# The same 722 operations of a two-head kernel, issued in another fixed order

## The chip, the cores and the metric

The kernel runs on one core of one Trainium2 chip. The metric is device time in microseconds (us) for one launch; the figure for a kernel is the median of several runs. A profile is one execution of its own, with its own time.

The engines are named as the profile names them: PE is TensorE's matmul row and PEld its weight loads, DVE is VectorE, ACT is ScalarE, POOL is GpSimd, SP is SyncE. [...] SP issues most of the DMAs here; POOL issues some.

## What is computed

The inputs have sequence length 2048 and width 640 in each of two halves; the output is 2048 x 1280.

```python
# half A: a diagonal complex recurrence between two projections
Bu = einsum("bld,pd->blp", x, B_bar)
h_t = Lam_bar * h_(t-1) + Bu_t
yA = 2 * einsum("blp,dp->bld", h, C).real + x * Dskip
# half B: a short convolution (4 taps), a gate, a long convolution (2048 taps, by FFT), a gate
kv = shift_conv(k) * v
yB = q * (irfft(rfft(kv) * rfft(ssm_k))[:2048] + kv * ssm_D)
```

## The kernel before

**The work is 722 named operations.** `Graph.op` records each with the engines that may run it, the values that it reads and writes, and the buffers that it uses. The string `ORDER` then lists all 722 names in one fixed sequence; `/A`, `/D`, `/G` and `/S` behind a name choose ACT, DVE, POOL or SP where there is a choice. `Graph.place` walks that string, gives each new buffer a slot, and `emit` issues the operations in that sequence. Each engine's program is therefore the sub-sequence of `ORDER` that falls to it.

**Half A.** `B00` to `B11` load B transposed; `xn0`, `xn1` load half of x, `px..` transpose it on PE and `ex..` copy it out; `x1..` load the other half with transposing DMAs. `dn0_j_h`, `dn1_j_h` (line 768, 10 matmuls each) project unit j; `e1_` copies the result out, `m1_` (line 776, 3 matmuls with the tables `set_n_h`) combines four time steps, `e3_` copies that out. `S0`, `S5` with `jw`, `jc`, `js`, `ja`, `scan`, `jv` run the coarse recurrence; `d1_j`/`a1_j` and `d0r_j`/`a0r_j` push it back down to single steps (one or three matmuls, then an addition on DVE). `ct..`/`ect..` build the output weights from C (loaded by `cn..`). `py0_ri` and `py1_ri` (lines 916 and 920, 13 matmuls each) project to the output, `ey_` copies out, `st_` stores.

**Half B** runs for five groups G of 128 channels, as a two-stage DFT written as matmuls. `kG`, `vG` are transposing loads issued by SP; `cv3`, `cs2`, `ca2` to `ca0`, `cm` are the four taps and the gate on ACT and DVE; `kvsG` stores the result to DRAM and `kvlG` loads it back in another layout. `hstG` loads the long filter, `dtapG` adds the skip term, for which `Dm0` clears and `Dm1` loads a small table. `s1h`, `s1k` (line 1019, 32 matmuls each) and `s2h`, `s2k` (line 1055, 16 each) are the forward transforms of filter and signal, each followed by a copy of 128x1024 out of PSUM (`e1h`, `e1k`, `e2h`, `e2k`). `pP`, `pQ`, `pY` multiply on DVE. `i2` (line 1111, 16 matmuls) and its copy `e3G.` begin the inverse, `ztG` is a transposing DMA (line 1118), `i1` (line 1147, 64 matmuls) ends it, `obGh` multiplies with q on DVE, and `obG` stores. `wm`, `ws`, `V` make the DFT tables.

**Buffers.** PSUM has four slots of two banks (tag `P`), and every product above takes one until the copy or addition behind it has read it. SBUF has six large slots (tag `8`) and seven smaller ones (tag `4`). The kernel before picks the slot whose last user ends first by the planner's own clock in `place`.

All copies out of PSUM carry line 350 when ACT does them and line 352 when DVE does; they are told apart by shape.

## Time and profile before

| what | value |
|---|---|
| median of 4 runs | 218.82 us |
| lowest and highest run | 218.65 and 220.35 us |
| the profiled execution: its own time | 220.35 us |
| the profiled execution: span from first to last instruction | 218.2 us |
| PE busy in the span | 194.4 us, 89% |
| DVE, ACT, POOL busy in the span | 175.5, 149.2, 29.0 us |
| 128x1024 copy out of PSUM on ACT, on DVE | 1025 and 1221 ns (83 and 17 of them) |
| SBUF-to-SBUF transpose (line 1118), issue to landing | 7.1 to 9.7 us |

The profiled execution took 2.15 us more than its span, and it is the slowest of the four runs, 1.53 us above their median. "Busy" of PE counts matmuls in flight, not the rate at which they stream. The chain of waits walks back from the last instruction to whatever released each step; "issue" in it is time in which an engine waited for nothing that the profile shows.

### The profile page before, as it was taken

To read this page: it belongs to the slowest core of one execution; us is meant where nothing else is said; L and a number is where in the kernel's file an instruction comes from. 1 tells how busy PE (TensorE), PEld (TensorE's weight loads), DVE (VectorE), ACT (ScalarE), POOL (GpSimd) and SP (SyncE) were. 2 spreads that over 40 slices of the span, in tenths; PEclk is the share of its full clock that TensorE was granted. 3 is DMA by queue.
4 is the path that set the end of the run, shared out by engine and by line. 5 is a ranking of instruction groups with operands and counts; after the bars stand their busy time and mean duration, and the time that the engine had idled before them with its cause. 6 is when DMAs were issued, how large, how long until landed. Compare 5 with 4: busy or idle time off the path is not lost.

```text
span 218.2 us, 8702 instructions
## 1 busy us (share of the span) xinstructions
PE 194.4 (89%) x3947; PEld 138.0 (63%) x3947; DVE 175.5 (80%) x264; ACT 149.2 (68%) x173; POOL 29.0 (13%) x41
## 2 busy tenths in 40 slices
PE   0839999997999799999698999996999989999992
PEld 0737554565765665655564777775777778778871
DVE  7578999889877999899788979955888878988240
ACT  2798689884797999699675675485484788560211
POOL 6116902381100000000000000210000000002020
PEclk9979999999999999999999999997999999999999
DMA  6999957999998443096907956799559980669934
GB/s 191 271 150 182 165 122 112 211 231 154 153 213 181 71 92 62 12 275 130 169 3 147 165 111 157 223 212 220 124 126 187 256 199 10 131 154 142 252 96 125
DMA packets 98751, 33.74 MB, mean 155 GB/s; under 512 B 94842, under 2 KB 96762, under 8 KB 98714
## 3 DMA queue, kind: packets, MB, share of 16 engines
q1 hardware_dynamic: 97580, 29.35, 69.0%
q0 software_dynamic: 1104, 3.84, 7.2%
q8 instruction: 31, 0.51, 1.0%
q14 instruction: 6, 0.05, 0.1%
q10 hardware_dynamic: 30, 0.00, 0.0%
HBM read 9.19 MB, written 7.86 MB: 78 GB/s over the span
## 4 chain that ended last, share of the span: by engine, by line
PE 67%; DVE 11%; ACT 11%; issue 5%; DMA 4%; DVEq 0%; ACTq 0%
PE ps L916 21%; PE ps L768 13%; PE ps L1055 8%; PE ps L1019 7%; PE ps L1147 5%; PE ps L1111 4%; PE ps L869 3%; ACT s L350 3%; DVE s L352 2%; DMA s<-in_A_x_dram 2%; PE ps L920 2%; DMA s<-kvd 2%; ACT xT L350 2%; ACT BC L350 2%; DVE M L535 2%
## 5 line engine op out<-in xcount | busy, mean ns | idle before, releaser
L350 ACT CAST s<-ps 128x1024 bf16<-128x1024 f32 x83 | 79.8, 1025 | 19.9 <-PE ps L1019 9.3
L768 PE MATMUL ps<-xT,BC 128*64 128x512 bf16 x400 | 46.4, 381 | 0.6 <-ACT s L350 0.3
L916 PE MATMUL ps<-BC,hb 128*128 128x320 bf16 x240 | 36.4, 299 | 0.0
L768 PEld LDWEIGHTS <-BC 128*64 128x64 bf16 x400 | 23.1, 110 | 18.7 <-issue 2.2
L1019 PE MATMUL ps<-R,s 64*64 64x128 bf16 x1280 | 24.0, 229 | 10.0 <-issue 4.3
L350 ACT CAST yo<-ps 128x640 bf16<-128x640 f32 x14 | 9.7, 693 | 32.4 <-PE ps L920 21.7
L1019 PEld LDWEIGHTS <-s 64*64 64x64 bf16 x1280 | 21.1, 115 | 13.9 <-issue 7.1
L916 PEld LDWEIGHTS <-hb 128*128 128x128 bf16 x240 | 22.0, 98 | 8.4
L352 DVE CAST s<-ps 128x1024 bf16<-128x1024 f32 x17 | 20.5, 1221 | 6.5 <-PE ps L1019 3.4
L1078 DVE TENSOR_TENSOR s<-s,s 128x2048 bf16<-128x2048 bf16 x20 | 24.4, 1222 | 0.9 <-ACT s L350 0.3
L873 DVE TENSOR_TENSOR hb<-ps,hb 128x512 bf16<-128x512 f32 x30 | 19.8, 686 | 4.7 <-PE ps L869 4.6
L1055 PE MATMUL ps<-s,Wre 128*64 128x128 bf16 x320 | 20.9, 221 | 2.8 <-DVE s L951 1.5
L1055 PEld LDWEIGHTS <-Wre 128*64 128x64 bf16 x320 | 18.0, 109 | 6.5 <-issue 5.3
L994 DVE TENSOR_TENSOR s<-s,s 128x2048 bf16<-128x2048 bf16 x15 | 20.3, 1354 | 0.4
L1055 PE MATMUL ps<-s,Wim 128*64 128x128 bf16 x320 | 20.6, 219 | 0.0
L986 ACT ACTIVATE s<-s,sk 128x2048 bf16<-128x2048 bf16 x9 | 18.1, 2014 | 3.3 <-DVE sk L660 2.5
L1055 PEld LDWEIGHTS <-Wim 128*64 128x64 bf16 x320 | 18.0, 110 | 0.3
L1154 DVE TENSOR_TENSOR s<-ps,s 128x1024 bf16<-128x1024 f32 x10 | 11.9, 1220 | 7.7 <-PE ps L1147 7.7
L350 ACT CAST hb<-ps 128x768 bf16<-128x768 f32 x16 | 12.6, 807 | 3.4 <-PE ps L768 3.4
L1078 DVE TENSOR_TENSOR s<-s 128x1024 bf16<-128x1024 bf16 x20 | 13.8, 689 | 0.3
L916 PE MATMUL ps<-BC,Qb 128*128 128x320 bf16 x80 | 13.0, 313 | 0.0
L988 DVE TENSOR_SCALAR s<-s,sk 128x2048 bf16<-128x2048 bf16 x11 | 12.2, 1117 | 0.1
(160 smaller groups left out, 269.5 us busy)
## 6 DMA issues: line engine op xcount, KB each, us to landing
s<-in_B_q_dram SPq DMA_DIRECT2D x5, 512.0 KB, 4.2
out_dram<-yo SPq DMA_DIRECT2D x15, 160.0 KB, 2.9
kvd<-s SPq DMA_DIRECT2D x4, 512.0 KB, 5.1
s<-kvd SPq DMA_DIRECT2D x4, 512.0 KB, 4.4
s<-in_B_ssm_k_dram POOLq DMA_DIRECT2D x3, 512.0 KB, 8.6
out_dram<-s SPq DMA_DIRECT2D x3, 512.0 KB, 5.5
s<-in_A_x_dram SPq DMA_DIRECT2D x2, 640.0 KB, 5.4
s<-in_B_ssm_k_dram SPq DMA_DIRECT2D x2, 512.0 KB, 4.3
```

Source lines behind the costliest of these rows:

```text
L350: self.nc.scalar.copy(out=out, in_=in_)
L352: self.eng[e].tensor_copy(out=out, in_=in_)
L768: nc.tensor.matmul(P[64 * ri:64 * ri + 64, b, :], lhsT=self.BT[:, k, ri, 64 * j:64 * j + 64], rhs=self.xT[:, k, hf, 2 * b:2 * b + 2, :].re ...
L873: v.tensor_tensor(out=hv(r), in0=self.P(p2)[:, 0, :].rearrange("p (h m) -> p h m", h=2), in1=hv(r), op=ALU.add)
L916: nc.tensor.matmul(P[:, part, 0:320], lhsT=hap(j), rhs=self.CT[:, j, c0:c0 + 320], start=(j == 0), stop=False)
L986: nc.scalar.activation(out=out, in_=k(j), func=ACT.Copy, scale=self.sk[:, G, j:j + 1])
L988: v.tensor_scalar_mul(out=out, in0=k(j), scalar1=self.sk[:, G, j:j + 1])
L994: op(f"ca{j}{G}{h}", {"DVE": dve_tt(W_)}, lambda e, c=c, tt=tt: v.tensor_tensor(out=c(), in0=c(), in1=tt(), op=ALU.add), r=[f"tm{G}{h}"], ...
L1019: nc.tensor.matmul(P[64 * ri:64 * ri + 64, r, 128 * b4:128 * b4 + 128], lhsT=d[64 * r:64 * r + 64, 4 * qd + b4, a0, :], rhs=self.R[64 * r: ...
L1055: nc.tensor.matmul(P[64 * pi:64 * pi + 64, ri, 128 * k4:128 * k4 + 128], lhsT=W[:, kp, pi, :], rhs=A[:, kp + 16 * pi, :], start=True, stop ...
L1078: v.tensor_tensor(out=o, in0=a, in1=b, op=op_)
L1154: v.tensor_tensor(out=o, in0=self.P(pt)[:].rearrange("p s (b a c) -> p a (s b) c", b=8, a=16), in1=o, op=ALU.mult)
```

## The change

The string `ORDER` is another sequence of the same 722 names. No name is added or removed, and no operation's body changes. 36 operations that had a choice move from ACT to DVE and 29 from DVE to ACT; seven table products `set_` change between DVE and POOL (four to POOL, three to DVE), as do three small steps (`kz0` and `dtap4` to POOL, `kz4` to DVE); and the issue of some DMAs moves between SP and POOL (to POOL: `q2`, `q4`, `kvs3`, `kvl4`, `st_01`; to SP: `hst0`, `kvl0`, `kvs1`, `ob3`, `ob4`, `st_32`).

`place` no longer keeps a clock of its own: a new buffer takes a slot never used before, or else the one whose last user stands earliest in the sequence. So the slots differ as well. `schedule` and `better`, which nothing called, are gone, and the constant 0.93 of `i1`, which `place` no longer reads, is 0.98.

The diff, cut to `place` and to the stretches of `ORDER` that are spoken of below:

```diff
         for word in text.split():
             name, _, e = word.partition("/")
             o = ops[name]
             o.eng = letter[e] if e else next(iter(o.alts))
-            assert o.deps <= done, name
-            s = free[o.eng]
-            for d in o.deps:
-                s = max(s, d.end + (0.0 if d.eng == o.eng and not d.dma else (0.3 if d.eng == "PE" else self.SEM)))
+            assert all(d in place for d in o.deps), name
             for b in o.bufs:
                 if b.slot is None:
-                    best = None
+                    ends = []
                     for i, own in enumerate(held[b.tag]):
-                        if own is not None and any(u not in done for u in own.users):
-                            continue
-                        t = 0.0 if own is None else max(u.end for u in own.users) + self.SEM
-                        if best is None or t < best[0]:
-                            best = (t, i)
-                    s = max(s, best[0])
-                    b.slot = best[1]
+                        if own is None:
+                            ends.append((-1, i))
+                        elif all(u in place for u in own.users):
+                            ends.append((max(place[u] for u in own.users), i))
+                    b.slot = min(ends)[1]
                     held[b.tag][b.slot] = b
...
-xn0 ld_lre J0 consts nrow xn1 J1 zero ld_ldt E0 pidx w0 ld_lim c4 nrowf hst1/G B00 E1 wi0 kz0/D bc kz1/G px00 wm0 px02 ex00/A
-px04 Dm0 w1 ex02/A Dm1/G px10 ex04/A par px12 ex10/A px14 p0 ex14/D B01 dtb ex12/A p1 fi w2 nrho ph mk rn k0 R dtap1/G Ct
-s1h10 trig scol s1h11 den s1h12 ld_sk/S e1h10/A rc B10 s1h13 ss e1h11/A dn0_4_0 set_1_0/D set_12_0/G e1h12/A dn1_4_0 B11
-set_1_1/G set_2_0/D e1h13/A dn0_0_0 e1_4_0/A set_2_1/G x100 dn0_1_0 set_3_0/D set_3_1/G dn0_2_0 x101 m1_4_0 sk set_8_1/G
+xn1 ld_lre J0 consts nrow xn0 J1 zero ld_ldt E0 pidx w0 ld_lim c4 nrowf hst1/G B00 E1 kz0/G wi0 bc Dm0 px12 Dm1/G w1 px10
+ex12/A px14 ex10/A wm0 px00 w2 par px02 p0 ex00/D B01 px04 ex14/D dtb mk k0 R ex02/A p1 fi dtap1/G ex04/A s1h13 nrho ph rn Ct
+s1h10 ld_sk/S scol B10 e1h13/D s1h11 trig den dn1_4_0 e1h11/A rc B11 ss e1h10/A dn0_4_0 set_3_0/D set_1_0/G x100 dn0_1_0
+set_2_0/G e1_4_0/D x101 dn0_2_0 sk cs200/D set_8_0/G m1_4_0 v0 cv300/A dn1_2_0 kz1/G set_12_0/D set_3_1/G e3_4_0/A dn0_7_0
...
+e3_7_0/D set_G_1/D dn1_0_1 set_G_0/D diagD dn0_1_1 dn1_1_1 e1_0_1/D kvl0/S hst0/S ws0 cs210/A wi1 m1_0_1 e1_1_1/D dn0_6_0 wm1
+m1_1_1 m1_9_0 e3_9_0/A ws1 v1 dn1_4_1 e3_1_1/D e3_0_1/D e1_6_0/D s1k03 s1k00 e1k03/D dn0_4_1 e1k00/D s1k01 dtap0/G V e1_4_1/A
...
-s1h20 ect40/A s1h21 jcv5 e1h20/A jv5 ect21/D jsv5 s1h22 e1h21/A s1h23 jav50 s1k20 e1h22/A jav51 s1k21 e1h23/D e1k20/A d1_7
-a1_7 d1_8 e1k21/A s1k22 a1_8 d00_7 s1k23 e1k22/A a00_7 d00_8 d1_0 e1k23/A a00_8 d1_1 a1_0 d01_8 s2k20 kz3/G k3 a1_1 s2k21
...
+a1_5 a1_6 ct40 ect31/A a1_7 s2k21 q0/S ect40/A s2k20 e2k21/A ct41 zt0 s2h21 s2h20 ect41/A e2h21/D d00_4 e2k20/A d00_1 a00_4
+d00_2 e2h20/A d00_7 a00_1 d00_0 a00_7 cs230/A d00_6 d00_9 a00_0 d00_5 a00_9 a00_5 s2h22 a00_2 s2h23 e2h22/A a00_6 py0_32
+e2h23/A pP20 i101 zt1 pQ20 py0_03 ob01 py1_03 pY20 i100 ca230 ey_03/A v3 i220 cs130/D d01_5 py1_32 e320/A ca130 st_03/S d01_2
...
-i223 ey_32/A i110 dtap3/G e323/A ob0/S st_32/G s1h30 ob10 s1h31 e1h30/A s1h32 e1h31/D s1h33 ob1/S e1h32/A d02_9 v4 a02_9 d01_6
-e1h33/A s1k30 a01_6 s1k31 e1k30/A s1k32 e1k31/D s1k33 e1k32/A py0_31 cs240/D e1k33/A ca240 py1_31 cs140/D s2k32 q2/S ca140
...
+s1k32 a02_7 s1k30 py0_10 e1k32/A ey_12/D ca240 st_12/S e1k30/A s2h31 s2h32 cs140/D e2h31/A py1_10 ca140 e2h32/A cs040/D s1k31
+ey_10/A s1k33 v4 ca040 py0_00 e1k31/A pP21 e1k33/A s2h33 st_10/S s2h30 pQ21 e2h33/A s2k33 py1_00 e2k33/A pY21 e2h30/A s2k32
+hst4/S ey_00/D i222 e2k32/A i223 cm40 st_00/S py0_13 e323/A kvs4/S e322/D s2k31 q4/G s2k30 e2k31/A py1_13 e2k30/D dtap4/G
+s1h40 ey_13/A s1h43 s1h41 e1h40/A st_13/S e1h43/D s1h42 kvl4/G e1h41/A py0_30 e1h42/A pP31 py1_30 pQ31 s2h43 ey_30/A s2h42
+pY31 s2h40 st_30/S e2h42/A py0_21 e2h43/D e2h40/A s1k42 zt2 pP30 s1k43 s1k40 e1k42/D py1_21 e1k40/A e1k43/D s1k41 ey_21/A
...
-e332/A s1k41 e333/D s1k42 e1k41/A s1k43 s2h43 e1k42/D e1k43/A py0_13 e2h43/A s2k42 pP30 q4/S pQ30 s2k40 e2k42/A s2k41 pY30
...
-d02_0 d02_6 a02_0 i130 zt4 a02_6 i131 ob30 py0_23 ob31 py1_23 ob20 ob3/G i121 ey_23/A py0_21 st_23/S ob21 py1_21 ob2/S i140
-ey_21/A i141 st_21/S ob40 py0_22 ob41 py1_22 ob4/G py0_20 ey_22/A st_22/S py1_20 ey_20/A st_20/S
+py1_31 pY40 e342/A i241 ey_31/A st_33/S i240 e341/D i120 st_31/S e340/A i121 ob20 zt4 ob21 py0_11 i131 ob2/S py1_11 ob31 i130
+ey_11/A py0_22 st_11/S ob30 i141 ob3/S i140 ob41 py1_22 ob40 py0_20 ey_22/D ob4/S st_22/S py1_20 ey_20/A st_20/S
...
-            op(f"i1{G}{h}", {"PE": 0.93}, f, r=["Ct", f"Zt{G}"], w=[f"p4{G}{h}"], bufs=[pt, Zt], due=due)
+            op(f"i1{G}{h}", {"PE": 0.98}, f, r=["Ct", f"Zt{G}"], w=[f"p4{G}{h}"], bufs=[pt, Zt], due=due)
```

## The prediction

> **What bounds the kernel now.** I read the page first (busy times, the PE clock, the chain of waits), then PE's own waits, then the chain in order of time, then busy time by stage.

> ```profile
> PE 194.4 (89%) x3947; PEld 138.0 (63%) x3947; DVE 175.5 (80%) x264; ACT 149.2 (68%) x173; POOL 29.0 (13%) x41
> PEclk9979999999999999999999999997999999999999
> ...
> q8 instruction: 31, 0.51, 1.0%
> ...
> PE 67%; DVE 11%; ACT 11%; issue 5%; DMA 4%; DVEq 0%; ACTq 0%
> ```

> ```profile
> PE ps L719 <- DMA s<-in_A_x_dram: 5.5, 1, 5.5
> PE ps L1019 <- issue: 4.3, 3, 1.9
> PE ps L1019 <- POOL s L941: 4.1, 1, 4.1
> ```

> ```profile
> 104.25 1.25 PE ps L1019 x75
> 105.51 1.54 issue
> 107.04 0.97 PE ps L1019 x53
> ...
> 147.91 1.89 issue
> 149.79 2.17 PE ps L1019 x87
> 151.97 2.32 PE ps L916 x10
> 154.42 1.36 PE ps L916 x10
> ...
> 177.75 0.87 issue
> 178.62 0.75 PE ps L1019 x39
> ```

> ```profile
> 23.70:55.60 31.90, 30.09 (x457) 17.75 (x459) 29.94 (x39) 26.82 (x32) 12.78 (x10) 1.00 0.94 166
> 63.50:120.50 57.00, 51.68 (x1005) 32.79 (x1001) 50.59 (x76) 47.56 (x58) 0.37 (x2) 1.00 0.58 118
> 120.50:175.20 54.70, 52.60 (x1176) 40.26 (x1174) 44.35 (x50) 34.26 (x36) 2.15 (x4) 0.97 0.81 179
> 175.20:214.20 39.00, 38.04 (x906) 30.17 (x898) 26.61 (x28) 17.39 (x20) 2.32 (x2) 1.00 0.68 141
> ```

> PE carries two thirds of the chain. Three of its pauses, 1.54 + 1.89 + 0.87 = 4.3 us, are "issue": no data was missing. All three fall inside a run of line 1019, and the second is followed by slow matmuls (87 in 2.17 us against 53 in 0.97; ten of line 916 in 2.32 against 1.36). The stage rows give PE, PEld, DVE, ACT, POOL in turn: up to 120 us PE and DVE are both nearly full; after that DVE has room and PE sets the pace.

> [...] The trace agrees on the block (31 fetches, 0.51 MB, 16 KiB each)[...]. I numbered PE's recorded instructions, two per matmul: the three pauses stand at instruction 3265, 5057 and 6337, which is 256k + 449 for k = 11, 18 and 23. So PE ran dry at a block's edge. Its block had been crossed in 5.0, 4.9 and 3.75 us; the packet itself takes about 1 us, most of the rest it waits to start. Elsewhere an edge was passed without a pause after 3.0 us. Hence: **a block that holds less than some 3 to 5 us of PE work stalls.** [...] Here it was halved for 3.41 us from 150.25 us[...].

> **The change, part by part.** Steps of PE, start to next start in this trace at full clock: s1 0.57 us (64 instructions), s2 and i2 0.55 (32), i1 1.13 (128), dn 1.08 (20), py 1.51 (26), m1 0.34, d1 0.33, d0 0.22. The total does not change. Adding these along each order shows where they fall.

> (1) *Blocks.* Before, the work per block is least at k = 17, 11, 18, 23: 2.5, 2.7, 2.7, 2.8 us (s1 steps side by side, as in `s1k30 .. s1k33`); three of these are the stalls. In the new order s1 and i1 stand between longer steps; the least are 2.9 (k = 3), 3.5 (k = 27, `i121 py0_11 i131`), then 4.2 and more. Gain: 1.89 + 0.87 in full; of the 1.54 at 105.5 little, since DVE is the tighter engine there. k = 3 lies among waits for copies that stretch it; k = 27 may cost 0 to 1.4, under the wait in (6).

> (2) *Slow clock.* With the pause at 147.9 its window goes: (2.17 - 87 x 0.0178) + (2.32 - 1.46) = 1.5 us.

> (3) *Head.* s1h waits for `dtap1`, that for `Dm1`, issued by POOL at 6.80 once DVE ran `Dm0` behind `wm0` (1.5 us). `Dm0` now stands ahead of `wm0`, so s1h can start about 1.5 us sooner. But next come the tables: `ss` ends at 18.0 on a chain through three ACT table loads of 1.28 that stays; then POOL makes `set_1_0` and `set_2_0` at 1.70 each, so `m1_4_0` starts near 21.6 with 1.7 us less PE work done (one dn, one s1) than before at 23.3. Gain 0, bounds -1.5 and +0.5.

> (4) *DVE and ACT.* Counted by the choices in the order and priced by their rows: DVE gets net one 1024 copy (1.22), three 768 (0.955), two 256 (0.42), one xT copy (1.2), one output copy (0.83), loses a tap (1.12) and a table: +4.6 us; ACT loses 3.9. Most of that comes early: from `m1_4_0` to the point at which 41.9 us of PE work are done, DVE has 26.6 us of listed work against 24.2. Before, it was 94% busy there (29.9 of 31.9). So (29.9 + 2.4)/0.94 = 34.4, and 0.7 for `s1k03`, whose `kvl0` now waits on SP for `kvs0` (5.1 + 4.4 us; `hst0`, `V`, `v1` queue behind it on SP, needed later): 21.9 + 35.1 = 57 where before it was 55.6. Bounds 55.5 and 61.

> (5) *The full middle.* DVE has then done 32.8 us of its list, before only 28. From 32.8 to 91.5 it took 60.2 us before for 58.7 of work, and PE now has 56.5 beside it. With 1 us for the tighter coupling: 57 + 61.2 = 118.2 at PE work 98.5, where the old order stood at 120.5. **Gain 2.3**, bounds +5 and -3. Inside lies a new wait: `zt0` now has 5.1 us of PE work, 8 of DVE, ahead of `i101`, and lands after 7.1 to 9.7; `zt1` takes the slot that `zt0` reads and waits for its landing. That is 0.5 to 1 us, most of it beside DVE's work.

> (6) *The end, PE-bound.* From PE work 98.5 to 150 the old order took 54.7, less 1.89 and 1.5: 51.3, plus 0.6 left of `i101`: 51.9. From 150 to 187.5: 39.0 - 0.9, plus two new waits. `v4` takes the slot that `cs140` and `cs040` read, so it is issued only after `cs040`: about 7.1 us (a transposing load) + 1.2 (`cm40` on DVE, where `e322`, `e2k30` queue behind) + 5.8 (`kvs4`) + 4.4 to 9.2 (`kvl4`, now on POOL, behind `q4` and `dtap4`) = 18.5 to 23.3 before `s1k42`, with 19.5 of PE work meanwhile: 1.2, bounds 0 and 4. And `zt4` is issued after `e340`: 1.0 + 8.4 against 9.05 of PE work up to `i141`: 0.4, bounds 0 and 1.7. Stage: 39.7. The DMAs moved to POOL are otherwise priced at nothing: POOL idles (29 of 218 us), and `q2`, `q4` have over 30 us before `ob`; if that cover went, each costs what its landing is late.

> Sum: 118.2 + 51.9 + 39.7 = 209.8, and the tail after the last py stays (last copy 0.69, store, landing; 4.0): span 213.8, that is 218.2 - 4.4. With 2.15 around it, 215.95 for an execution like the profiled one (220.35), which was 1.53 above the median. About two thirds of that excess I take to be pauses that the new order would not have had: 215.95 - 1.0 = **215.0 us**, against the median 218.82.

> **Rivals.**
> *A, the forecast*: fetch pauses and the slow window go, new waits give back a part: 215.0, its own range 211.5 to 217.5. Chance 0.65.
> *B, new waits take the place*: (6) at its upper ends (+2.8 + 1.3) keeps the time near 219. For it: the chain through `v4` has no slack on paper; against: each landing used is a median or worse. Chance 0.15.
> *C, the fetch stays dear*: if an edge needs 5 us everywhere, blocks 3, 8, 10, 11, 15, 17, 26, 27 lack 2.1 + 0.7 + 0.8 + 0.5 + 0.6 + 0.5 + 0.7 + 1.5 = 7.4, about half under other waits: 218.7. Against: edges were passed at 3 us. Chance 0.06.
> *D, slower*: DVE becomes the bound in the first 60 us. Between `e1_0_1` and `e1k00` ACT holds `ws0`, `cs210`, `ws1` (3.45 + 2.0 + 3.45) while seven copies fall to DVE, and units 0, 1, 6, 9 hold all four PSUM slots. If that wedge costs over 6 us beyond (4), the middle starts after 63 and the sum passes 221: some 222. Against: ACT can take `ws0` early, having little before it. Chance 0.14.

> About 1% is what a measurement of this kernel can tell from no change: 216.6 to 221.0. Faster by more: A below 216.6 and a sliver of C, 0.60. Within: the rest of A, B, most of C and a part of D, 0.25. Slower: most of D, a part of B, 0.15. The range, 211.5 to 220.0, takes in A, C and most of B.

> **What will show it.** Right if no "issue" pause over 0.5 us on line 1019 is left after 60 us and the clock row shows no dip near slice 28; if the last third from PE work 98.5 takes under 93 us (old 93.7); if `s1k42` and `i141` show waits for a DMA of 0 to 2 us. Step 3 is wrong if `m1_4_0` starts far from 21.6; steps 4 and 5 if PE work 41.9 and 98.5 are not reached near 57 and 118. The forecast fails if pauses merely move to other edges, or if DVE idles between 57 and 118 us.

## The result: no gain, and what the profile after shows

Over 43 executions of the changed kernel and 64 of the kernel before, the medians are **219.85 us** after (218.09 to 222.12) and 219.43 us before (216.92 to 223.07). The ratio is **1.0038, interval 1.0020 to 1.0056**: within 1%, where 215.0 was forecast. Every ratio and interval here leaves out the executions that took over 1.5% more than the fastest of the same kernel, while the medians take in all. The profiled execution of the changed kernel took 218.88 us (span 216.4), 1.0 below its own median, while that of the kernel before had been 1.5 above the median then known. So the two traces alone show a gain of 1.5 us that the medians don't have.

The page after: busy times, the PE clock row, the instruction queue and the head of the chain of waits, then two groups of the waits of PE (us in total, times, longest).

```profile
PE 194.7 (90%) x3947; PEld 135.9 (63%) x3947; DVE 175.3 (81%) x269; ACT 146.7 (68%) x166; POOL 31.5 (15%) x42
PEclk9999999999999999999999999999999999999999
...
q8 instruction: 30, 0.49, 0.9%
...
PE 68%; DVE 10%; DMA 8%; ACT 7%; issue 6%; POOL 1%; POOLq 0%; ACTq 0%
```

```profile
PE ps L881 <- POOL s L803: 5.1, 2, 3.4
...
PE ps L1009 <- DMA s<-s: 1.2, 1, 1.2
```

The pauses "issue" ahead of the s1 matmuls (line 1019 before, line 881 after) are gone from the waits of PE, and the clock row has no dip. In their place stand two waits. Line 881 behind POOL is 3.4 us in the head, where the old order waited 4.1, and **1.7 us in the middle**, which is new. Line 1009 behind a transpose is `i141` behind `zt4`. Of the pauses without missing data one is left, 0.44 us in `py0_20` near the end.

The chain in order of time shows both (start, us, what):

```profile
135.88 0.28 issue
136.16 0.57 POOL out_dram L791
136.73 6.12 issue
142.90 0.27 POOL s L803
143.21 1.12 PE ps L881 x64
...
195.55 9.59 DMA s<-s
205.18 2.21 PE ps L1009 x128
...
210.36 0.44 issue
```

"POOL s L803" is `dtap3`, which adds the skip term to the filter that `hst3` loads. The 6.12 us ahead of it are named "issue" only because the chain found no event there; the waits of POOL put 6.2 us down to the load `hst3`, and `q2`, next on POOL, was issued only behind it, at 143.42. The next matmuls are `s1h33` and its fellows.

Why is `hst3` late? First the DMA issues of the changed kernel from 128 to 156 us (issuer, count, size, median us from issue to landing), then the same view of the kernel before, then when the changed kernel issued them (start, us of the issuer).

```profile
out_dram<-s SPq DMA_DIRECT2D x2, 512.0 KB, 9.7
...
s<-in_B_ssm_k_dram POOLq DMA_DIRECT2D x1, 512.0 KB, 8.8
s<-kvd SPq DMA_DIRECT2D x1, 512.0 KB, 10.0
```

```profile
out_dram<-s SPq DMA_DIRECT2D x2, 512.0 KB, 6.1
...
s<-in_B_ssm_k_dram POOLq DMA_DIRECT2D x1, 512.0 KB, 5.6
```

```profile
130.85 2.49 SPq L816 DMA_TRANSPOSE s<-in_B_k_dram  x1
133.39 0.64 POOL L860 DMA_DIRECT2D kvd<-s  x1 [45.91 <-DVE s L813]
134.02 1.20 POOL L800 DMA_DIRECT2D s<-in_B_ssm_k_dram  x1
134.26 3.83 SPq L1019 DMA_DIRECT2D out_dram<-s  x2
...
138.13 4.92 SPq L862 DMA_DIRECT2D s<-kvd  x1
```

Within 5 us the new order starts the transposing load `k4`, the store `kvs3`, the load `hst3` (second row) and two output stores of 512 KB, `ob1` and `ob0` (line 1019). `hst3` takes 8.8 us; before, where `ob0` and `ob1` went out at 142.9, behind the reload `kvl3`, it took 5.6. Here `kvl3` (last row) comes behind the stores on SP and takes 10.0. The stretch of the two orders, with what lies between left out:

```diff
-kvs3/S ... hst3/G ... ob00 kvl3/S ... dtap3/G ... ob0/S ... ob10 ... ob1/S
+ob10 ... k4 kz4/D kvs3/G ... ob11 hst3/G ... ob00 ob1/S ... ob0/S ... kvl3/S ... dtap3/G
```

### The profile page after: what moved, and what is told of

It is laid out like the page before. It is cut to its first block, busy times and chain, and to the rows that moved or that the text cites. A ratio compares the mean times of both kernels' runs of the same rounds, so it can differ in the third digit from the quotient of the medians.

```text
span 216.4 us, 8689 instructions
## 1 busy us (share of the span) xinstructions
PE 194.7 (90%) x3947; PEld 135.9 (63%) x3947; DVE 175.3 (81%) x269; ACT 146.7 (68%) x166; POOL 31.5 (15%) x42
## 4 chain that ended last, share of the span: by engine, by line
PE 68%; DVE 10%; DMA 8%; ACT 7%; issue 6%; POOL 1%; POOLq 0%; ACTq 0%
PE ps L778 18%; PE ps L630 17%; PE ps L881 9%; PE ps L917 8%; DMA s<-s 4%; ACT s L212 4%; PE ps L973 4%; DMA Dm<-in_B_ssm_D_dram 4%; PE ps L1009 3%; PE ps L638 2%; DVE hb L735 2%; PE ps L782 2%; PE ps L715 2%; PE ps L731 1%; DVE s L214 1%
## 5 line engine op out<-in xcount | busy, mean ns | idle before, releaser
L630 PE MATMUL ps<-xT,BC 128*64 128x512 bf16 x400 | 47.2, 386 | 0.5 <-ACT Qb L212 0.5
L778 PE MATMUL ps<-BC,hb 128*128 128x320 bf16 x240 | 36.6, 300 | 0.1
L630 PEld LDWEIGHTS <-BC 128*64 128x64 bf16 x400 | 21.7, 111 | 20.4 <-issue 3.3
L214 DVE CAST s<-ps 128x1024 bf16<-128x1024 f32 x18 | 21.7, 1222 | 11.5 <-PE ps L881 5.3
L212 ACT CAST yo<-ps 128x640 bf16<-128x640 f32 x13 | 9.0, 691 | 29.5 <-PE ps L782 28.4
L778 PEld LDWEIGHTS <-hb 128*128 128x128 bf16 x240 | 21.9, 98 | 9.4 <-issue 0.4
L881 PEld LDWEIGHTS <-s 64*64 64x64 bf16 x1280 | 20.2, 111 | 10.6 <-POOL s L803 5.5
L848 ACT ACTIVATE s<-s,sk 128x2048 bf16<-128x2048 bf16 x10 | 20.0, 2015 | 5.6 <-DVE sk L522 2.8
L735 DVE TENSOR_TENSOR hb<-ps,hb 128x512 bf16<-128x512 f32 x30 | 19.2, 685 | 4.8 <-PE ps L731 4.8
L397 POOL TENSOR_TENSOR M<-E,ss 128x640 bf16<-128x640 bf16 x8 | 14.0, 1776 | 4.1 <-DVE ss L387 4.1
L1009 PE MATMUL ps<-Ct,s 128*64 128x64 bf16 x640 | 11.6, 196 | 1.9 <-DMA s<-s 1.2
L1009 PEld LDWEIGHTS <-s 128*64 128x64 bf16 x640 | 10.9, 113 | 3.0 <-DMA s<-s 1.3
```

The costliest lines, as they stand in the source:

```text
L212: self.nc.scalar.copy(out=out, in_=in_)
L214: self.eng[e].tensor_copy(out=out, in_=in_)
L397: self.eng[e].tensor_tensor(out=mt[:, js, :].rearrange("p j (r i) -> p j r i", r=2), in0=E[:].rearrange("p (a b i) -> p a b i", a=1, b=1). ...
L630: nc.tensor.matmul(P[64 * ri:64 * ri + 64, b, :], lhsT=self.BT[:, k, ri, 64 * j:64 * j + 64], rhs=self.xT[:, k, hf, 2 * b:2 * b + 2, :].re ...
L735: v.tensor_tensor(out=hv(r), in0=self.P(p2)[:, 0, :].rearrange("p (h m) -> p h m", h=2), in1=hv(r), op=ALU.add)
L778: nc.tensor.matmul(P[:, part, 0:320], lhsT=hap(j), rhs=self.CT[:, j, c0:c0 + 320], start=(j == 0), stop=False)
```

## The experiments

Line numbers in the kernels of the experiments are higher by one (line 882 is line 881 of the changed kernel, line 1020 is line 1019 of the kernel before), with the moved edges by seven; the second trace of an unchanged kernel keeps its lines.

Below, "the table" is this: I gave each group of matmuls the duration that the lower third of its kind has in these traces (179.1 us in all), and took that sum off the time at which each group starts. What grows between two points of PE work is time in which PE stood or ran slowly. Where two orders do different work at a boundary, a few tenths of a difference between them can come from the boundary alone.

| PE work, us | before | before, 2nd trace | after | after, 2nd | end edit | end edit, 2nd | stores edit | both edits | both, 2nd | moved edges |
|---|---|---|---|---|---|---|---|---|---|---|
| 0 to 60 | 16.3 | 16.3 | 14.4 | 14.2 | 13.3 | 13.4 | 14.3 | 13.3 | 16.0 | 16.3 |
| 60 to 114 | 9.1 | 9.1 | 9.6 | 9.6 | 9.5 | 9.6 | 9.6 | 9.6 | 9.6 | 10.5 |
| 114 to 132 | 5.0 | 2.6 | 3.6 | 5.5 | 5.5 | 5.5 | 3.2 | 2.9 | 3.2 | 4.4 |
| 132 to 168 | 3.0 | 3.2 | 1.9 | 1.9 | 1.9 | 1.9 | 1.9 | 1.9 | 1.9 | 4.4 |
| 168 to the last py | 0.1 | 0.8 | 2.3 | 2.0 | 1.0 | 1.7 | 2.2 | 2.8 | 1.0 | 2.1 |

### Second traces of the two orders, unchanged

> The kernel before, profiled once more. Theory 1 (the three fetch pauses and the slow clock window after 147.9 us belong to every execution): pauses of 1 to 2 us in the s1k2 and s1k3 groups again, and PE at half clock for some 3 us after the second. Rival (they were chance of the one profiled execution, which was 0.9 us above the median): pauses under 0.5 us, span near 217.

Measured, kernel before: 218.82 us, span 216.6. The same three pauses stand at the same three edges, but shorter: 1.14, 1.09 and 0.97 us where the first trace had 1.54, 1.89 and 0.87. No slow clock followed; 114 to 132 cost 2.6 us instead of 5.0.

```profile
PE ps L1019 <- issue: 3.2, 3, 1.1
```

> The changed kernel, profiled once more. Theory 1 (a wait of 3.4 us for dtap3 took most of the gain, and a slow clock window after it takes the rest in most executions): the wait before s1h33 is again 2 to 4 us, and PE runs at half clock for 3.4 us after it, which the first profile did not have; span about 217.5. Rival (the first profile was typical in its clock): span 216.4, no half-clock window after 18 us. A ratio of 1.00 to 1.005 to the kernel before in either case.

Measured, kernel after: median 220.11 us in 20 executions, ratio 1.0062 (1.0035 to 1.0090), traced span 217.8. Its waits of PE and its clock row:

```profile
PEclk9957999999999999999999999988999999999998
```

```profile
PE ps L881 <- POOL s L803: 6.2, 2, 4.0
```

The wait ahead of `s1h33` is 6.2 - 4.0 = 2.2 us here, and at 144.9 us a stretch of 3.41 us at half clock follows, the two 8s in the row. 114 to 132 costs 5.5 instead of 3.6. So the order loses time at `hst3` each time, and the execution profiled first was the milder one. In the order before the pauses at the edges recur too; their size, and whether the clock falls, does not.

### The wait of s1h3 filled with other PE work

```diff
-i221 dtap3/G ... s1h33 ... s1h32 s1h30 ... s1h31 ... q2/G ... py0_12 ... py1_12 ... cv340/A ... s1k32 ... s1k30 py0_10
+i221 dtap3/G ... py0_12 ... py1_12 ... s1h33 s1h32 ... s1h30 ... py0_10 s1h31 q2/G e1h31/A cv340/A q3/S s1k32 s1k30
```

> The changed order with the four s1h3 products put behind py0_12, py1_12 (and py0_10 in between), so that 3.5 us more of PE work lie ahead of the one that waits for dtap3. Theory 1: the wait of 3.4 us shrinks to under 0.5 and the slow window behind it goes: 2.5 to 4.5 us less than the changed kernel, ratio 0.98 to 0.99 to the kernel before. Rival (the time is set by DVE or by the DMAs behind it, the wait only shows it): the wait moves to s1k32 or to a later step, and the time stays within 1 us of the changed kernel.

Measured: 220.47 us, ratio 1.0092 (1.0063 to 1.0122). The wait at `s1h33` did go, and 2.2 us of PE pause appeared at `s2h32` some 10 us later, with the half clock behind it from 154.6:

```profile
PE ps L918 <- ACT s L213: 2.6, 3, 2.2
```

```profile
149.78 1.01 ACT L213 CAST s<-ps 128x1024 bf16<-128x1024 f32 x1 [1.66 <-PE ps L882]
150.69 2.00 ACT L849 ACTIVATE s<-s,sk 128x2048 bf16<-128x2048 bf16 x1
152.59 3.74 ACT L213 CAST s<-ps 128x1024 bf16<-128x1024 f32 x4
```

The second view is ACT's timeline: the s1 copies now come late and meet the tap `cv340` (2.00 us, line 849) ahead of the four copies that PSUM waits for. My edit moved the pause instead of removing it; it says nothing for or against the crowd of transfers.

### The kernel before with its short blocks filled

```diff
-s1k31 e1k30/A s1k32 e1k31/D s1k33 e1k32/A py0_31
+s1k31 e1k30/A py0_31 s1k32 e1k31/D s1k33 e1k32/A
...
-e333/D s1k42 e1k41/A s1k43 s2h43 e1k42/D e1k43/A py0_13
+e333/D py0_13 s1k42 e1k41/A s1k43 s2h43 e1k42/D e1k43/A
```

> The order before, with py0_31 moved ahead of s1k32 and py0_13 ahead of s1k42, so that the two blocks of instructions that ran dry at 147.9 and 177.8 us hold 1.5 us more work. Theory 1: both pauses and the slow window go: 1.9 + 0.9 + 1.5 = 4.3 us, ratio 0.98 to 0.985. Rival (the pauses are mostly chance, or the time comes back as waits for copies): within 1 us of the kernel before.

Measured: 219.03 us, ratio 1.0028 (1.0000 to 1.0057): none of the 4.3 us. In its trace the pause near 178 is gone and that near 149 shrank from 1.09 to 0.80 (against the second trace of before), but the one near 107, whose block was not touched, came out at 1.84 and drew a slow stretch at 107.2; the third, of 0.87, stands at an edge near 56 us, where neither trace of the kernel before has a pause.

```profile
PE ps L1020 <- issue: 3.5, 3, 1.8
```

So the sum of the pauses in one trace, 4.3 us, is not what an edit that fills two of three blocks gets back in the median.

### Both kernels' edges put to the test: the same order, other block edges

What the traces show of a block: the instruction queue q8 carried 31 packets of 16 KiB before and 30 after, for 7894 recorded instructions of PE and PEld, that is one for 255 and one for 263; the three pauses of the trace before lie 1792 and 1280 instructions apart, 7 and 5 times 256. In the blocks ahead of these pauses the packet began 2.6, 2.6 and 1.2 us after the block's first instruction and took 1.0, 1.0 and 1.25 us, and PE went on 1.5, 1.4 and 1.4 us after its end. So what the prediction says of the wait to start, most of the rest, holds for the first two alone.

The edit adds 66 matmuls of 10x10 that nobody reads, half ahead of `px12`, half behind `px04`, where PE waits anyway. Nothing else changes its place, but each edge of a 256-instruction block falls 132 instructions elsewhere.

```diff
+        def f_pad(e):
+            for c in range(33):
+                nc.tensor.matmul(self.P(self.par)[:, 1, 0:10], lhsT=self.ident[0:10, :], rhs=self.ident[0:10, 0:10],
+                                 start=True, stop=True)
+        for k in range(2):
+            op(f"pad{k}", {"PE": 1.5}, f_pad, r=["ident"], w=["pad"], bufs=[self.par], due=-25)
```

> The changed kernel with 66 small matmuls (10x10 outputs that nobody reads) added in the head, half ahead of px12 and half behind px04, where TensorE waits anyway. They leave the order of all else as it is, but move every edge of the 256-instruction blocks by 132 instructions: the TensorE work within a block falls to 2.3 to 2.7 us for four blocks (one near 47 to 60 us, one near 130, one near 165, one near 195), and 3.3 to 3.5 for two more, where the changed kernel has 2.9 and 3.5 as its least. Theory F (a block with less than some 4 us of work ends in a pause for instruction fetch): four to six pauses of 0.7 to 1.6 us appear at the new edges, 3.0 to 5.5 us more than the changed kernel, ratio to the kernel before 1.016 to 1.028. Rival C (the pauses of the kernel before come from somewhere else, and the fetch only lies beside them): not more than 0.5 us, ratio 1.002 to 1.007.

Measured: **225.07 us, ratio 1.0272 (1.0208 to 1.0337)**, some 5 us above the changed kernel, at the upper end of what the fetch theory asked. The waits of PE:

```profile
PE ps L1016 <- issue: 3.0, 3, 1.8
...
PE ps L789 <- issue: 2.5, 2, 1.4
...
PE ps L888 <- issue: 1.7, 2, 1.3
```

Seven pauses, 7.2 us, without missing data, on three different lines. Counted by instructions, all seven stand at the same place of a block as the three of the kernel before: the cause is the place of the edge, not the kind of operation. The added matmuls themselves did not delay the head: `m1_4_0` starts at 21.3 us, in the changed kernel at 21.5. Some 2 of the 7.2 us came back, since the wait for `hst3` is 0.9 us here and that for `zt4` is gone. This is the clearest run of the study: but for the added matmuls one and the same order took 5 us more for where its edges lie.

### More cover for zt4 at the end

```diff
-py0_22 st_11/S ob30 i141 ob3/S i140 ob41 py1_22 ob40 py0_20 ey_22/D ob4/S st_22/S py1_20
+py0_22 st_11/S ob30 ob3/S py1_22 i141 ey_22/D i140 ob41 st_22/S ob40 py0_20 ob4/S py1_20
```

> The changed kernel with i141 and i140 put behind py1_22 (ey_22, st_22, ob41 and ob40 follow them), so that 1.5 us more of TensorE work lies ahead of the matmuls that wait for the transpose zt4. Nothing else moves. Theory G (the fetch gain is there, and is given back in the wait for hst3 and in the wait for zt4 at the end): the wait of 1.2 to 1.4 us ahead of i141 goes, and the time falls by 1.0 to 1.5 us against the changed kernel (ratio to the kernel before near 0.998). Rival T (the tail takes it back, because ob4 is stored later): no more than 0.3 us gained (ratio 1.002 to 1.007). Rival N (nothing was given back, the typical kernel before has no fetch pauses worth the name): also a gain of 1.0 to 1.5 us here; only the next runs tell it from theory G.

Measured: 220.05 us, ratio 1.0067 (1.0036 to 1.0099). The wait for `zt4` is gone from the trace, and the last row of the table fell from 2.3 to 1.0, yet the median shows nothing. A later store of `ob4` is not the reason: from the end of the last matmul to the end of the span both traces take 3.85 us. A second trace:

> The order with i141 and i140 behind py1_22 once more, unchanged, for a second trace of its end. From the start of s1k42 to that of py1_20 its first trace took 34.8 us (the changed kernel 36.1 and 35.8). Theory K (with the wait for zt4 gone, the last block of 256 instructions, i141, i140 and most of py0_20, holds only some 3.2 us of work, and its fetch becomes the new wait in most executions): a pause of 1 to 2 us without missing data within py0_20, and 35.8 to 36.6 us. Rival: as in the first trace, a pause below 0.5 us and 34.7 to 35.2 us; then the gain at the end is real in most executions and was lost elsewhere.

Measured: 219.12 us; 35.5 us from `s1k42` to `py1_20`, between the two expectations, with a pause of 1.2 us in `py0_20`:

```profile
PE ps L783 <- issue: 1.2, 1, 1.2
```

Its companion, the order with the stores edit below, gave 1.85 us of pause in its first trace and 0.3 in its second. So the last block, which now holds `i141`, `i140` and most of `py0_20`, pauses 0.3, 1.2, 1.9 and 0.3 us in four traces: the last row of the table moves by anything from +0.5 to -1.3 us, less than these medians can tell.

### hst3 issued earlier

```diff
-ob10 py0_01 cm30 s2k23 k4 py1_01 kz4/D kvs3/G e2k23/A ob11 hst3/G
+ob10 py0_01 cm30 s2k23 hst3/G k4 py1_01 kz4/D kvs3/G e2k23/A ob11
```

> The changed kernel with the load hst3 issued ahead of the transpose k4 in the order: it takes another buffer, free some 2.5 us sooner, and stands ahead of kvs3 in the GpSimd queue; the order of the compute engines stays as it is. Theory G: hst3 is issued near 131 instead of 134, dtap3 near 140 instead of 142.9, the wait of s1h33 (2.4 to 2.9 us in the two profiles) falls below 0.5, and of this 1.5 to 2.2 us arrives at the end (kvl3 lands near 148 and is next); ratio to the kernel before 0.994 to 0.998. Rival R (the stage is held by another chain, as the run with the later s1h3 suggests): the wait goes and the time stays within 0.5 us of the changed kernel, ratio 1.002 to 1.006, with new waits of the same size within the next 15 us.

Measured: 221.84 us in 6 executions, ratio 1.0125 (1.0068 to 1.0182): slower than the kernel before, which neither theory had. Its interval overlaps that of the changed kernel's second measurement (1.0035 to 1.0090), so that it is slower than the changed kernel is not shown. Its profiled execution took 227.20 us. With the end edit as well:

> Both edits, hst3 early and i141, i140 behind py1_22. Theory G: they add up, 2.5 to 3.7 us below the changed kernel, ratio to the kernel before 0.987 to 0.993. Rivals: 1.0 to 1.5 us from the end alone (ratio 0.997 to 0.999) or nothing (1.002 to 1.007).

Measured: 221.05 us, ratio 1.0046 (1.0010 to 1.0083), which is what its second rival said (nothing gained). The trace of the latter, issues from 128 to 156 us and the waits of PE:

```profile
s<-in_B_ssm_k_dram POOLq DMA_DIRECT2D x1, 512.0 KB, 6.5
kvd<-s POOLq DMA_DIRECT2D x1, 512.0 KB, 12.5
...
s<-in_B_k_dram SPq DMA_TRANSPOSE x1, 13.4
```

```profile
PE ps L882 <- DMA s<-kvd: 3.9, 1, 3.9
```

`hst3` came in time (landing 6.5 us after issue), and the wait of `s1h33` went. But `k4` took the buffer that `hst3` had had, was issued 2.2 us later (133.05), and now stood in the crowd itself: `kvs3`, which now also stands behind `hst3` in the GpSimd queue, needed 12.5 us instead of 3.6, so `kvl3` was issued at 146.2 instead of 138.1, and `s1k32` waited 3.9 us for it. One load less in the crowd, another one more: the wait moved to whoever came last. That made the crowd itself the suspect. Two of its members are the stores `ob1` and `ob0`, whose data no later step reads.

### The two stores behind the reload

```diff
-kvs3/G e2k23/A ob11 hst3/G py0_02 ob00 ob1/S ey_01/A st_01/G d01_7 ob0/S d01_4 ... kvl3/S
+kvs3/G e2k23/A ob11 hst3/G py0_02 ob00 ey_01/A st_01/G d01_7 d01_4 ... kvl3/S ob0/S ob1/S
```

> The changed kernel with the two 512 KB stores ob0 and ob1 moved on SyncE from ahead of the reload kvl3 to behind it, the side of it on which the kernel before has them. No compute instruction changes its place. Theory D (the load hst3 and the reload kvl3 are late because the order puts two big stores and kvs3, hst3 and k4 in flight together, between 131 and 136 us): hst3 lands in 5.5 to 7 us instead of 8.8 to 9.3, dtap3 runs near 140 to 141, the wait of s1h33 falls from 2.4 to 3.6 us to below 1, kvl3 is issued near 137 and lands by 144 instead of 148, no half-clock stretch follows near 143 to 146, and the time falls by 2 to 4 us against the changed kernel: ratio to the kernel before 0.988 to 0.998. Rival Q (the crowd only moves on): the stores now lie under q2, q3 and the copy cs240, which takes the buffer that ob0 frees; the wait comes back on q2, cs240 or s1k3, and the time stays within 1 us, ratio 0.999 to 1.007.

Measured: **217.97 us, ratio 0.9966 (0.9939 to 0.9993)**, in one batch with a kernel before at 219.03. No compute instruction moved. One thing besides the stores' place did change: `ob0` now stands ahead of `ob1`, so by the rule of `place` `q2` takes the buffer that `ob0` frees and `cs240` the one that `ob1` frees; in the changed kernel it is the other way round. The issues of the stretch and when they came:

```profile
out_dram<-s SPq DMA_DIRECT2D x2, 512.0 KB, 6.8
...
s<-in_B_ssm_k_dram POOLq DMA_DIRECT2D x1, 512.0 KB, 6.4
```

```profile
133.90 1.20 POOL L801 DMA_DIRECT2D s<-in_B_ssm_k_dram  x1
136.03 0.57 POOL L792 DMA_DIRECT2D out_dram<-yo  x1 [0.94 <-ACT yo L213]
136.84 0.38 SPq L863 DMA_DIRECT2D s<-kvd  x1
137.35 5.13 SPq L1020 DMA_DIRECT2D out_dram<-s  x2
```

`hst3` stands in the same place of the same queue and lands after 6.4 us instead of 8.8; the wait ahead of `s1h33` is gone from the waits of PE. Over all traces with the order of `kvs3` and `hst3` unchanged: with the stores ahead 8.8, 9.3, 9.3, 9.4, 8.9 and 8.4 us, with them behind 6.4, 6.2 and 6.4. For these 2 to 3 us that decides for the crowd and against the GpSimd queue. The 0.6 to 0.8 us that are left above the 5.6 of the kernel before can be either; no run separates them.

Part of the wait came back elsewhere, as the rival said. The first line is of the waits of PE, the second of ACT's timeline:

```profile
PE ps L918 <- ACT s L213: 1.4, 2, 1.2
```

```profile
147.18 3.90 ACT L849 ACTIVATE s<-s,sk 128x2048 bf16<-128x2048 bf16 x2 [2.00 <-DMA out_dram<-s]
```

`cs240` on ACT waited 2.00 us for the later of the two stores, whose buffer it takes; the copies behind it came late, and PE stood 1.22 us at `s2h31` (0.97 and 1.30 us in the two traces with both edits). So 1.0 to 1.3 us came back of a pause of 1.7 to 2.25. What did not come back is the half clock. Every execution lists its mean granted clock. The clock records of the first traces of both kernels have the values 1 and 0.5 alone; if the others have no other value, an estimate of mine, twice the missing share times the span is the time at half clock. On average that is 4.6 us here (22 executions) and 4.2 with both edits (14), against 7.2 and 6.8 for the changed kernel (44 and 20) and 6.6 to 7.3 for the kernel before (35 to 48 in a batch). The same edit with `ob1` ahead of `ob0` was not run.

The gain, 0.7% to 1.0% or 1.6 to 2.1 us by the two ratios of the changed kernel, is at the lower end of what was expected; the expected 2 to 4 us took the 2.2 us of wait and the slow stretch as typical, and the table has the difference at 0.4 to 2.6 us.

### Both edits

> The same with i141 and i140 behind py1_22 as well, so that both places of waiting that the profile of the changed kernel names are taken away. Theory D: another 1.0 to 1.3 us (the stretch from s1k42 to the end was that much shorter in the trace of the run with this edit alone), ratio to the kernel before 0.983 to 0.993, faster than both kernels. Rival: the end's gain does not reach the median, as in that run; then the same ratio as the run with the stores alone.

Measured: 218.23 us, **ratio 0.9943 (0.9916 to 0.9971)**, by ratio the best of all orders here, though its interval overlaps that of the stores alone, so that the end's share is not shown. A second trace:

> The order with the stores behind kvl3 and i141, i140 behind py1_22 once more, unchanged. Its first trace took 36.6 us from s1k42 to py1_20, with a pause of 1.85 us in py0_20. Theory K: again 1 to 2 us of pause there, 35.8 to 36.6 us. Rival: below 0.5 us of pause and 34.7 to 35.2 us.

Measured: 218.72 us, 34.8 us from `s1k42` to `py1_20`, pause 0.3: the rival's numbers. This execution lost its time in the head instead, 16.0 us up to PE work 60 against 13.3 in the first trace of the same order.

## Why the prediction was wrong

The forecast 215.0 against 219.85: the difference is 4.85 us, and by the forecast's own terms it splits into 2.6 (stage from 98.5 to 150) + 0.3 (time around the span, 2.48 instead of 2.15) + 1.0 (the subtraction at the end) + 1.0 (the profiled execution lies that far below its median). Part of the last 1.0 need not be the order's: the median of the kernel before rose by 0.6 as well, from 218.82 in four executions to 219.43 in 64.

**(1) Blocks: right in mechanism, too large in size.** No "issue" pause over 0.5 us was left in the trace after, as step and signs said, and moving the edges cost 5 us. But the terms 1.89 and 0.87 came from one execution; the second trace of the same kernel (218.82 us) had 1.09 and 0.97 there, 0.7 us less, and the edit that took one of these two pauses away and shortened the other gained nothing in the median.

**(2) Slow clock: right once, not in the median.** The 1.5 us for the halved stretch stood in the sum as if every execution of the kernel before had it. The second trace has none. And the new order draws one itself: three of the four traces with its middle have it, behind the wait for `hst3`. Over all executions it ran no less at half clock than the kernel before (the averages above).

**(3) Head: held.** `m1_4_0` started at 21.5, forecast 21.6.

**(4), (5) DVE, ACT and the full middle: held.** PE work 41.9 was reached at 55.9 (forecast 57), 98.5 at 118.7 (forecast 118.2).

**(6) The end: the step that failed.** Priced: a wait of 1.2 at `s1k42` through `v4`, which measured 0, and 0.4 at `i141`, which measured 1.2 and lay within its bounds; the stage from 150 came out at 39.2 against 39.7. Not priced: 98.5 to 150 took 54.45 us instead of 51.9, and 51.9 left next to nothing for new waits beside 51.5 us of PE work. So the sign "under 93 us" for the last third failed too: 93.65. The sentence at fault is "The DMAs moved to POOL are otherwise priced at nothing". I looked at whether POOL was idle enough to issue them, and at the two loads with cover, not at what else is in flight when they land; and the stores `ob1`, `ob0`, which the order moved on SP from behind `kvl3` to ahead of it, I did not count at all, as moved steps' DMAs have to be. Their cost was not in SP's queue alone but in the landing of `hst3`, where 5.6 became 8.4 to 9.4, and of `kvl3`. The table shows it from 114 to 132: 5.5 us in three of four traces, 2.9 to 3.2 once the stores were put back. Nor is the crowd the whole of it. By the count of work used in the prediction, 98.5 to 150 took 56.2 us in those three traces and still 53.6 to 53.9 with the stores put back, 1.7 to 2.0 above the forecast. Two waits stand in it that no step had priced: the 1.0 to 1.3 us through `cs240`, and 0.6 us at `i110` behind an addition on DVE, which the changed order has in all its traces.

**The last subtraction counted twice.** "About two thirds of that excess I take to be pauses that the new order would not have had": the pauses that the forecast removes were already taken out in steps (1) and (2). An execution that is slow because of what the change removes needs no second correction, and 216.0 would have been the consistent number.

**The rivals.** B is what happened, new waits in the place of the old, and near its 219; but the largest was at `hst3`, which it did not name. Of the two that it named `v4` cost nothing and `zt4` 1.2 us, so B was right in kind and only in part in place. C fell with the pauses absent after; D with PE work 41.9 reached at 55.9 and the first 60 us of PE work taking 1.9 us less.

Shown by an edit: the crowd, worth 1.6 to 2.1 us of the median when it was undone, and the effect of edges, which were moved. Only argued: what filling the blocks of the old order is worth in the median, since the one edit that did so showed no gain; why a pause at the same edge is 0.3 us once and 1.9 another time, and what the changed orders spend around the span (2.4 against 2.2 us on average over their executions).

## What to carry to other kernels

When an order moves, list every DMA that moves in each queue, and for the critical loads ask not only when they are issued but what else is in flight between issue and landing; a store whose data nobody waits for belongs behind a load that somebody does (here worth 1.6 to 2.1 us of the median), but look up who takes the buffer that it frees: here `cs240` did, and waited for the store. With short PE steps of many instructions, count PE work between block edges, and know that added instructions move the later edges: 132 of them in the head did so here, and the time rose by some 5 us. And take a second trace before pricing a pause: what one execution lost is not what the median loses.

## What the runs showed of the hardware

**The landing of `hst3` changed with its company.** The same 512 KB load from the same place of the same queue landed after 6.2 to 6.4 us or 8.4 to 9.4, depending on whether two 512 KB stores went out beside it. A 512 KB store took 3.6 us or 12.5, but there its place in the queue had changed as well, so that what company did to it alone is not shown.
